# Later reciprocals, later sums: moving four small pieces of work in a fused attention and feed-forward kernel

## The chip, the cores and the metric

The kernel runs on one core of one Trainium2 chip. The metric is the device time of one execution in microseconds. Before the change three runs took 1024.36, 1024.68 and 1027.38 us; the median is 1024.68.

## The reference

Three stages follow each other. The first is causal attention over 4 batches, 8 heads, 576 positions and 64 values a head, with a bias from running sums:

```
s_pos  = max(s, 0);  cum = cumsum(s_pos)            # per head, along the positions
scores = q @ k.T / 8 + min(-(cum_q - cum_k), 0)     # -1e9 above the diagonal
attn   = exp(scores - max) / (sum + 1e-9)
x      = attn @ v                                   # heads side by side: 2304 x 512
```

The second stage is `(h - tanh(h)) @ w_out` with `h = x @ w_in` (512 to 2048 to 512). The third is `((x @ w1) * (x @ w2)) @ w3 @ w_out` (512 to 1024 to 512). All is in float32.

## The kernel before

The first part of the kernel runs attention and half of the second stage, woven into each other. The second part runs the other half, multiplies w3 by the last weights, and runs the third stage. Weights come in as pairs of 32-bit words of 64-bit numbers; VectorE puts each tile together with three instructions (L76, L78, L80), ScalarE rounds it and GpSimd takes the difference (L62, L63). Two buffers hold raw tiles, one for a w_in tile (raw_win) and one for a w_out tile (raw_wout) at a time, so that a load waits for the conversion before it.

Attention works on 32 pairs of heads. A pair of kind A covers the first 256 queries in one unit of work; a pair of kind B covers the other 320 queries in three units (B1, B2, B3). Pairs 0 to 3 are of kind A and pairs 4 to 7 of kind B, all of batch 0. From pair 8 on the kinds take turns. `k0` is the step at which a pair's first unit is scored; its units are two steps apart, and `ke` is the step of the last.

The order on TensorE is written by hand. Each piece of work is entered with `at(step, order, function)`; steps run upward, and the order number sorts within a step. Filling matmuls (`warm`, L187, three a step) stand in steps 0 to 11. For a pair the entries are:

- `scores` (L201, for batch 0 also L216) at the unit's step; `minimum` (row maxima, L228 to L232) and `exps` (L257, L258 or L261) one step later.
- `invert` (L304, L305) at `ke + 2`: VectorE adds 1e-9 to the row sums and takes reciprocals into `rw`.
- `turn` (L309) at `ke + 3`: TensorE transposes `rw` into a bank named `pri`.
- `store` (L314, L316) at `ke + 4`: ScalarE copies `pri` to `rt`, and SP writes it to a small tensor `rd` in device memory.
- `spread` (L322) at `ke + 6`: SP reads `rd` back twice, each over 64 partitions, into `rb`.
- `transposes`, `evacuate` and `products` (L272, L281, L298) some 5 to 9 steps after the scores; `finish` (L335) at `ke + lag + 3`, where `lag` is 5 for the first four pairs and 7 for the rest: VectorE multiplies the product by `rb` into `xy`.

`scores`, `transposes`, `turn`, the products of most pairs and `queries` take their bank from one pool of five (`ps_a`). A bank comes free when its last reader is done.

For batch 0 the bias is made on TensorE. It needs `rel2`: for each of five chunks of queries the running sums less the sum at the chunk's start, in a rounded part (L556) and a correction (L557). VectorE makes all ten at the start, in the order of chunks 0, 1, 3, 4, 2. Pairs 0 to 3 use chunks 0 and 1; pair 4 uses chunk 3 at step 8, chunk 4 at step 10 and chunk 2 at step 12. `queries` (L562, L565) transposes the running sums into a bank `pcq` and copies them to `cq`, which batches 1 to 3 use from step 30 on.

The second stage enters steps as units of six matmuls (`ffn`). When a block of 256 tokens may begin follows from the `finish` steps: the first at step 14, the second at step 40. The code spreads the units over the steps between.

VectorE, ScalarE, GpSimd and SP are not ordered by hand: a planner gives each a fixed order from its own estimate of when each instruction can run, and the engines then take their instructions in that order.

Of the kernel before, what the change touches and what calls it, by code (L numbers as in the profile page):

```python
# [37 lines left out]
def tile_kernel(ctx: ExitStack, tc: tile.TileContext, qk, v, s, w_in, w_out, w1, w2, w3t, w_o2, outT):  # L38
# [65 lines left out]
    with ExitStack() as actx:  # L104
# [355 lines left out]
        def at(step, order, fn, *args):  # L460
            when.setdefault(step, []).append((order, len(when.get(step, ())), fn, args))
# [10 lines left out]
        for p in pairs:  # L472
            n, k0 = p.n, k
            lag = 5 if p.first and p.early else 7
            for m, j in enumerate(p.units):
                k = k0 + 2 * m
                for i in NEED[j]:
                    at(max(k - 2, start), 5, bias, p, i)
                    if not p.first:
                        at(max(k - 1, start + 1), 0.2, causal, p, i)  # L480
                at(k, 4, scores, p, j)
                at(k + 1, 1, minimum, p, j)
                at(k + 1, 2.5, exps, p, j)
                for e in range(2):
                    at(k + e + lag, 2, transposes, p, j, e)
                    at(k + e + lag + 1, 1.5, evacuate, p, j, e)
                at(k + lag + 2, 8, products, p, j)
            ke = k0 + 2 * len(p.units) - 2
            k = ke + 2
            at(ke + 2, 5.5, invert, p)  # L490
            at(ke + 3, 2.4, turn, p)
            at(ke + 4, 1.2, store, p)
            at(ke + 6, 3.9, spread, p)
            fin = ke + lag + 3
            at(fin, 2.6, finish, p)
            if p.hp == H // 2 - 1:
                avail.append((S * p.b + (BLK if p.early else S), fin))

            if n > 1 and (p.early or p.first):
                q = p if p.first else pairs[n + 1]  # L500
                at(max(k0 - 6, start + 1), 4.2, load, p, q, "load")
                at(max(k0 - 2, start + 1), 4.3, load, p, q, "load_v")
                if not p.first:
                    at(k0 - 5, 4.4, load, p, pairs[n + 1], "load_cum")
# [43 lines left out]
        for z in range(2):  # L548
            for y in range(2):
                nc.gpsimd.tensor_copy(rel2[z][2 * NH:, 512 * y:512 * y + 512], zeros[2 * NH:])  # L550
        for i in (0, 1, 3, 4, 2):
            z, r = REL[i]
            w = min(P * (i + 1), S)
            base = cum[:, CH0[i] - 1:CH0[i]] if i else 0.0
            hi, lo = rel2[z][:NH, r:r + w], rel2[z][NH:2 * NH, r:r + w]
            nc.vector.tensor_scalar(out=hi, in0=cum[:, :w], scalar1=base, scalar2=None, op0=ALU.subtract)  # L556
            nc.vector.scalar_tensor_tensor(out=lo, in0=cum[:, :w], scalar=base, in1=hi.bitcast(F32), op0=ALU.subtract, op1=ALU.subtract)  # L557

        def queries():
            pt = ps_a.tile([P, 512], F32, tag="s", name="pcq")  # L560
            for i in range(5):
                nc.tensor.transpose(pt[:PW[i], NH * i:NH * i + NH], cum[:, CH0[i]:CH0[i] + PW[i]], ident[:NH, :NH])  # L562
            for i0, i1 in ((0, 3), (3, 5)):
                pw = PW[i0]
                nc.vector.tensor_scalar(out=cq[:pw, i0:i1], in0=pt[:pw, NH * i0:NH * i1].rearrange("p (i g) -> p i g", g=NH),  # L565
                                        scalar1=-1.0, scalar2=None, op0=ALU.mult)

        at(12, 5.2, queries)

        ff = ffn()  # L570
        alive = True
# [193 lines left out]
```

## Time and profile before

| | |
|---|---|
| median of three runs | 1024.68 us |
| profiled execution | 1030.51 us |
| its span | 1028.2 us |
| TensorE busy (PE) | 974.8 us, 95% |
| VectorE busy (DVE) | 524.5 us, 51% |
| ScalarE busy (ACT) | 394.7 us, 38% |
| GpSimd busy (POOL) | 253.8 us, 25% |
| mean granted TensorE clock | 0.972 |

Times inside the profile count from the start of the span. A row of the timeline has start, duration, engine, line, operation and tiles; the square bracket at its end is the idle time of the engine before it and what ended that. A granted clock of 1.00 is full speed.

### The profile page before, as it was taken

How to read it: one execution, taken by the hardware profiler on the slowest of the kernel's cores; microseconds unless marked ns; L12 is line 12 of the kernel's file. 1: busy time of each engine (PE TensorE's matmuls, PEld its weight loads, DVE VectorE, ACT ScalarE, POOL GpSimd, SP SyncE). 2: the span in 40 equal slices, each digit the busy share in tenths (PEclk: the TensorE clock that was granted, in tenths of full speed). 3: DMA queues.
4: the chain of work that ended last, by engine and by line, in shares of the span. 5: the costliest groups of instructions: out<-in, count | busy, mean ns of one | idle time of the engine just before them, and what ended most of it. 6: DMA issues, size and time to landing. Idle time of an engine off the chain costs nothing.

```text
span 1028.2 us, 15378 instructions
## 1 busy us (share of the span) xinstructions
PE 974.8 (95%) x5809; PEld 795.6 (77%) x5809; DVE 524.5 (51%) x1173; ACT 394.7 (38%) x978; POOL 253.8 (25%) x249
## 2 busy tenths in 40 slices
PE   5877898999999999999988999999999999999998
PEld 2544676668787878999867878889888888888898
DVE  8885645755656664642696575657312213122121
ACT  2555566676666654311432333232212112121121
POOL 3332565654433330100332322232101001000000
PEclk7879899999999999999998999999999999999999
DMA  6656745652222310135358361629800101001010
GB/s 201 205 184 231 237 148 175 207 205 83 94 73 99 106 67 31 62 101 186 118 164 272 103 221 61 211 101 341 335 1 1 41 1 41 1 1 42 1 41 21
DMA packets 46234, 123.64 MB, mean 120 GB/s; under 512 B 4977, under 2 KB 16913, under 8 KB 46161
## 3 DMA queue, kind: packets, MB, share of 16 engines
q1 hardware_dynamic: 41840, 106.94, 30.6%
q10 hardware_dynamic: 4320, 15.73, 4.6%
q8 instruction: 45, 0.74, 0.3%
q14 instruction: 29, 0.23, 0.1%
HBM read 92.09 MB, written 30.56 MB: 119 GB/s over the span
## 4 chain that ended last, share of the span: by engine, by line
PE 49%; DVE 6%; DMA 3%; ACT 1%; issue 1%; POOL 0%; SPq 0%; ACTq 0%; POOLq 0%; DVEq 0%
PE oc L100 10%; PE a L100 10%; PE b L100 10%; PE hb L100 6%; PE yb L100 6%; PE w3o L100 4%; PE h L100 2%; PE y L402 2%; DVE cvt_w L78 1%; DVE glb L63 1%; DVE x L63 1%; DMA raw_w<-in_w3t 1%; DVE cvt_w L76 1%; DMA win<-wf_d 1%; DVE cvt_wo L78 1%
## 5 line engine op out<-in xcount | busy, mean ns | idle before, releaser
L100 PEld LDWEIGHTS h<-xhl,win 128*128 128x128 f32 x864 | 111.5, 193 | 30.7 <-issue 12.6
L100 PE MATMUL h<-xhl,win 128*128 128x256 f32 x864 | 126.8, 293 | 8.5 <-DVE th L433 7.1
L712 DVE TENSOR_TENSOR pc<-b,pc 128x512 f32<-128x512 f32 (+1 forms) x40 | 25.5, 637 | 163.3 <-PE b L100 163.3
L100 PE MATMUL hb<-x,win 128*128 128x512 f32 (+1 forms) x480 | 106.8, 369 | 1.5 <-DMA win<-wf_d 1.5
L100 PE MATMUL a<-y,w 128*128 128x512 f32 (+1 forms) x480 | 106.4, 368 | 0.0
L100 PE MATMUL b<-y,w 128*128 128x512 f32 (+1 forms) x480 | 106.0, 368 | 0.0
L100 PE MATMUL yb<-ghb,wout 128*128 128x512 f32 (+1 forms) x320 | 99.1, 376 | 5.6 <-ACT ghb L62 3.7
L100 PEld LDWEIGHTS hb<-x,win 128*128 128x128 f32 x480 | 84.5, 189 | 17.0 <-DMA win<-wf_d 1.7
L100 PE MATMUL oc<-phc,w3s 128*128 128x512 f32 (+1 forms) x320 | 96.7, 368 | 0.0
L100 PEld LDWEIGHTS b<-y,w 128*128 128x128 f32 x480 | 84.3, 189 | 15.0
L100 PEld LDWEIGHTS a<-y,w 128*128 128x128 f32 x480 | 84.2, 189 | 14.9
L180 POOL TENSOR_SCALAR pr<-cb,cq 128x384 f32<-128x384 f32 (+1 forms) x48 | 86.2, 1813 | 9.5 <-DMA cb<-cum_d 5.7
L402 PE MATMUL y<-gh,wout 128*128 128x256 f32 x576 | 88.1, 292 | 0.0
L402 PEld LDWEIGHTS y<-gh,wout 128*128 128x128 f32 x576 | 74.7, 191 | 6.5 <-issue 5.1
L261 ACT ACTIVATE pr<-pr,nm 128x128 f32<-128x128 f32 (+2 forms) x120 | 71.4, 598 | 20.5 <-DVE nm L239 20.1
L63 POOL TENSOR_TENSOR y<-xy,y 128x512 fp32r<-128x512 f32 (+1 forms) x10 | 13.5, 1356 | 248.8 <-ACT y L62 248.6
L711 ACT COPY pc<-a 128x512 f32<-128x512 f32 (+1 forms) x40 | 21.8, 544 | 134.8 <-PE a L100 134.8
L100 PEld LDWEIGHTS yb<-ghb,wout 128*128 128x128 f32 x320 | 59.6, 192 | 17.8 <-ACT ghb L62 4.3
L201 PE MATMUL s_B<-qk 64*96 64x512 f32 (+2 forms) x256 | 60.2, 531 | 12.2 <-ACT pr L257 6.7
L100 PEld LDWEIGHTS oc<-phc,w3s 128*128 128x128 f32 x320 | 58.5, 189 | 9.9
L100 PE MATMUL yb<-glb,wout 128*128 128x512 f32 (+1 forms) x160 | 59.7, 377 | 1.7 <-DVE glb L63 1.7
L62 ACT CAST phc<-pc 128x512 fp32r<-128x512 f32 (+1 forms) x40 | 23.1, 578 | 93.2 <-DVE pc L712 93.2
(129 smaller groups left out, 1646.6 us busy)
## 6 DMA issues: line engine op xcount, KB each, us to landing
qk<-in_qk SPq DMA_DIRECT2D x16, 576.0 KB
raw_w<-in_w3t SPq DMA_DIRECT2D x16, 512.0 KB
raw_w<-in_w SPq DMA_DIRECT2D x16, 512.0 KB
wg_d<-park_w SPq DMA_DIRECT2D x16, 512.0 KB
w<-wg_d SPq DMA_DIRECT2D x16, 512.0 KB
raw_win<-in_w_in ACTq DMA_DIRECT2D x15, 512.0 KB
raw_wout<-in_w_out ACTq DMA_DIRECT2D x15, 512.0 KB
cb<-cum_d SPq DMA_DIRECT2D x12, 576.0 KB
```

What stands on the lines that cost most here:

```text
L62: (hi or nc.scalar.copy)(dst_hi, src)
L63: (lo or nc.gpsimd.tensor_sub)(dst_lo, src, dst_hi.bitcast(F32))
L76: nc.vector.tensor_scalar(out=t, in0=r3[:, :, 1], scalar1=3, scalar2=0x3FFFFFFF, op0=ALU.logical_shift_left, op1=ALU.bitwise_and)
L78: nc.vector.scalar_tensor_tensor(out=t, in0=r3[:, :, 0], scalar=29, in1=t, op0=ALU.logical_shift_right, op1=ALU.bitwise_or)
L100: nc.tensor.matmul(ps, a, b, start=first and n == 0, stop=last and n == 2, skip_group_check=skip)
L180: nc.gpsimd.tensor_scalar(out=t[:pw, e, :w], in0=p.cb[:pw, e, :w], scalar1=c, scalar2=0.0, op0=ALU.add, op1=ALU.min)
L201: latest[0] = nc.tensor.matmul(ps[e][:PW[i], o:o + k1 - k0], x[:, 0, CH0[i]:CH0[i] + PW[i]], x[:, 1, k0:k1], start=(i, k0, k1, o) == UNITS ...
L261: nc.scalar.activation(t[:pw, :], t[:pw, :], AF.Exp, bias=m, scale=-1.0, accum_out=p.sums[:pw, e, c:c + 1])
L402: nc.tensor.matmul(o, wout[f][:, z, P * c:P * c + P], x, start=f == 0 and n == 0 and c % 2 == 0, stop=f == F1 - 1 and n == 2, skip_group_c ...
L711: nc.scalar.copy(t[:, :n], pa[:, :n])
L712: nc.vector.tensor_mul(t[:, :n], pb[:, :n], t[:, :n])
```

## The change

`turn` moves from `ke + 3` to `ke + 5`, `store` from `ke + 4` to `ke + 6`, into the step of `spread`. `finish` of the first four pairs moves one step. With it the first block of the second stage may begin at step 15. Of the ten instructions on `rel2`, the six of chunks 3, 4 and 2 are entered at steps 2, 3 and 4, and `queries` moves from step 12 to step 22.

```diff
-            at(ke + 3, 2.4, turn, p)
-            at(ke + 4, 1.2, store, p)
+            at(ke + 5, 2.4, turn, p)
+            at(ke + 6, 1.2, store, p)
             at(ke + 6, 3.9, spread, p)
-            fin = ke + lag + 3
+            fin = ke + lag + (4 if p.first and p.early else 3)
...
-        for i in (0, 1, 3, 4, 2):
+
+        def relative(i):
             z, r = REL[i]
             w = min(P * (i + 1), S)
             base = cum[:, CH0[i] - 1:CH0[i]] if i else 0.0
             hi, lo = rel2[z][:NH, r:r + w], rel2[z][NH:2 * NH, r:r + w]
             nc.vector.tensor_scalar(out=hi, in0=cum[:, :w], scalar1=base, scalar2=None, op0=ALU.subtract)
             nc.vector.scalar_tensor_tensor(out=lo, in0=cum[:, :w], scalar=base, in1=hi.bitcast(F32), op0=ALU.subtract, op1=ALU.subtract)
+
+        for i in (0, 1):
+            relative(i)
+        for z, i in enumerate((3, 4, 2)):
+            at(2 + z, 5.6, relative, i)
...
-        at(12, 5.2, queries)
+        at(22, 5.2, queries)
```

## Rows read from the trace of the kernel before

**Rows 1.** The page's slices of 25.7 us, in tenths: TensorE busy, granted clock.
```profile
PE   5877898999999999999988999999999999999998
...
PEclk7879899999999999999998999999999999999999
```

**Rows 2.** TensorE's waits, 0 to 130 us: total us, times, longest.
```profile
PE pri L309 <- DVE nm L232: 8.0, 1, 8.0
...
PE s_B L201 <- issue: 4.6, 1, 4.6
```

**Rows 3.** Timeline of TensorE around the first transposition of reciprocals.
```profile
20.88 0.45 PE L309 MATMUL pri<-ident,rw 128*96 128x128 f32 x1 [7.98 <-DVE nm L232]
21.12 1.49 PE L187 MATMUL spare<-zeros,identb 128*128 128x512 bf16 x3
22.53 1.65 PE L201 MATMUL s_A<-qk 64*128 64x128 f32 x8
```

**Rows 4.** Stretches: length, busy us of PE, PEld, DVE, ACT, POOL, clock, DMA, GB/s.
```profile
10.00:54.00 44.00, 30.70 (x174) 18.01 (x172) 36.68 (x83) 19.77 (x62) 15.03 (x15) 0.79 0.61 190
...
20.90:33.50 12.60, 11.37 (x49) 6.99 (x50) 10.70 (x22) 6.49 (x24) 4.67 (x4) 0.64 0.57 173
...
250.00:450.00 200.00, 199.40 (x1615) 168.45 (x1614) 115.36 (x366) 108.18 (x302) 58.78 (x63) 1.00 0.22 71
```

**Rows 5.** Timeline of VectorE before pair 0's reciprocals.
```profile
17.57 0.43 DVE L76 TENSOR_SCALAR cvt_win<-raw_win 128x512 uint32<-128x512 uint32 x1 [2.81 <-DMA raw_win<-in_w_in]
...
20.65 0.17 DVE L305 RECIPROCAL rw<-rw 128x4 f32<-128x4 f32 x1
```

**Rows 6.** VectorE's waits, 10 to 54 us.
```profile
DVE cvt_win L76 <- DMA raw_win<-in_w_in: 4.9, 4, 2.8
```

**Rows 7.** Tile rel, VectorE's instructions: ns least, median, most; first and last start; forms.
```profile
L556 DVE TENSOR_SCALAR rel<-cum x5: 215/402/501, 5.8 to 7.0; 32x128 fp32r<-32x128 f32 x1, 32x256 fp32r<-32x256 f32 x1, 32x512 fp32r<-32x512 f32 x1, 32x576 fp32r<-32x576 f32 x1
L557 DVE SCALAR_TENSOR_TENSOR rel<-cum,rel x5: 280/602/801, 7.5 to 9.5; 32x128 fp32r<-32x128 f32 x1, 32x256 fp32r<-32x256 f32 x1, 32x512 fp32r<-32x512 f32 x1, 32x576 fp32r<-32x576 f32 x1
```

**Rows 8.** Timeline around pair 5's first scores.
```profile
54.03 0.38 DVE L565 TENSOR_SCALAR cq<-pcq 128x96 f32<-128x96 f32 x2
...
54.51 1.99 PE L201 MATMUL s_B<-qk 64*96 64x512 f32 x2 [4.60 <-issue]
...
58.13 2.02 PE L201 MATMUL s_B<-qk 64*96 64x512 f32 x2 [1.63 <-ACT pr L257]
```

**Rows 9.** Timeline of ScalarE's queue: first and last of six requests for raw_win.
```profile
12.77 0.38 ACTq L67 DMA_DIRECT2D raw_win<-in_w_in  x1
...
52.08 0.33 ACTq L67 DMA_DIRECT2D raw_win<-in_w_in  x1
```

**Rows 10.** Timeline: a pair's reciprocals copied, stored, spread and used.
```profile
22.82 0.24 ACT L314 COPY rt<-pri 4x128 f32<-4x128 f32 x1
...
37.34 0.41 DVE L335 TENSOR_TENSOR xy<-pv,rb 128x256 f32<-128x256 f32 x1
...
41.19 0.64 SPq L316 DMA_DIRECT2D rd<-rt  x1
...
45.73 1.11 SPq L322 DMA_DIRECT2D rb<-rd  x2
...
160.22 0.64 SPq L316 DMA_DIRECT2D rd<-rt  x1
...
166.63 1.12 SPq L322 DMA_DIRECT2D rb<-rd  x2
...
176.74 0.42 DVE L335 TENSOR_TENSOR xy<-pv,rb 128x256 f32<-128x256 f32 x1 [1.29 <-PE pv L298]
```

**Rows 11.** Timeline: a conversion on VectorE beside a subtraction on GpSimd.
```profile
21.39 1.27 POOL L63 TENSOR_TENSOR win<-cvt_win,win 128x512 fp32r<-128x512 f32 x1 [5.50 <-ACT win L62]
21.50 1.71 DVE L80 SCALAR_TENSOR_TENSOR cvt_wout<-raw_wout,cvt_wout 128x512 uint32<-128x512 uint32 x1
```

**Rows 12.** Timeline of TensorE: a later transposition of reciprocals.
```profile
181.61 0.28 PE L309 MATMUL pri<-ident,rw 128*96 128x128 f32 x1 [2.03 <-DVE rw L305]
```

## The prediction

> **What bounds the kernel now.** I read the page's slices first, then TensorE's waits, then the timeline of the places they name, then stretches of both engines. Of the forty slices TensorE's busy share is five to eight tenths in six of the first seven, and nine in nearly all that follow; the granted clock is below full in the same early slices [rows 1]. From 250 to 450 us it works 199.4 of 200 us [rows 4]. So nothing later makes up for time lost early, and time won early reaches the end, as long as the stages between carry it on.
>
> The largest wait of TensorE is one: 8.0 us before the transposition of pair 0's reciprocals (pri) [rows 2]. Its order is written by hand, and at step 3 this transposition stands ahead of the scores of pair 2. The engine stands still for 7.98 us up to 20.88, and pair 2's scores start at 22.53 [rows 3]. What it waits for is VectorE: the reciprocal runs at 20.65, behind a conversion that had itself waited 2.81 us for its raw weights [rows 5]. After the stall the clock is low: the mean is 0.64 from 20.9 to 33.5 us, between the levels 1.2 and 2.4 GHz [rows 4].
>
> But VectorE is the fuller engine there. From 10 to 54 us it works 36.7 of 44 us, TensorE 30.7 [rows 4]. VectorE takes its instructions in order, and 4.9 us of its 7.3 idle us are waits for the next raw_win [rows 6]. The conversions and the row maxima before step 12 are the same work after the change. So the reductions of pair 4's last chunk can come earlier by 7.3 us at most if the same work stands before them, however early TensorE has the scores ready.
>
> **The change part by part.** The profiled execution took 1030.51 us (span 1028.2 and 2.3 around it), 5.83 above the median of 1024.68. I work in us saved against that execution and take the same number from the median.
>
> *Transposition at the pair's last step plus 5 in place of 3.* TensorE's next work at step 4, three filling matmuls and pair 2's scores, no longer has the reciprocal ahead of it. It needs two of the five banks that pairs 0 and 1 hold or leave free, and gets the second when pair 0's exponentials are done, which the reciprocal needs as well. Removed: up to 7.98 us of stall. Late next is VectorE, so the value is what fills VectorE's idle time, counted after the next edit.
>
> *Sums of chunks 3, 4 and 2 at steps 2, 3 and 4.* These are three subtractions and three corrections (L556, L557). By median and longest of each five, the 384-wide ones take 0.40 and 0.60 us, the 576-wide ones 0.50 and 0.80, the 512-wide ones about 0.47 and 0.72: 3.5 us [rows 7]. They now stand before the first conversion and the first row maxima. Without them both come up to 3.5 us earlier, the second load of raw_win is asked for earlier, and the moved work has a place in the 2.81 us that VectorE idles [rows 5]. From both sides: a gain of 3.5 us if all finds idle time, and a loss of 3.5 if the planner of the engines' order puts it in front of the row maxima of pair 1. I take 2.8, the size of that gap, since the gap stands right behind the work of that time.
>
> *Together, up to step 12.* Of the 7.3 us, 2.8 are spent; 4.5 are left. Pair 2's row maxima no longer wait for TensorE and may fill such gaps, but a wait for raw_win holds everything behind it. I take a third: 1.5 us (between 0 and 4.5).
>
> *The queries at step 22 in place of 12.* TensorE waits 4.60 us before pair 5's first scores, which start at 54.51 when VectorE has copied pcq (54.03) out of its bank [rows 2, 8]. Without pcq they start up to 4.6 us earlier. But the second half waits for a bank of pair 4 whose exponentials (L257) are still to come, and starts at 58.13; that stays. Left is the copy's 0.38 us, which stood in VectorE's order before the last row maxima were scaled: 0.3 us. At step 22 the bank is taken while two chunks, not three, have theirs; cost between 0 and one such copy, taken as 0.
>
> *Later pairs.* At 181.61 TensorE waits 2.03 us for another reciprocal (L305) [rows 12]. Two steps later that wait is over. VectorE's backlog stays, so I count half: 1.0 (0 to 2.03).
>
> *The moved work beside GpSimd.* The corrections run now while GpSimd rests. Beside the conversions they can meet its subtractions of weights. One VectorE conversion beside such a subtraction took 1.71 us against GpSimd's 1.27 [rows 11], while a correction of the same kind takes 0.28 to 0.80 alone [rows 7]. Between 0 and three times 1.27, 3.8 us. GpSimd works 4.67 of the 12.6 us from 20.9 to 33.5 [rows 4], a share of 0.37; three corrections that meet it by that share and wait half a subtraction each pay 0.7, which I take.
>
> The Trainium skill ("SBUF — State Buffer", section "Who interferes with whom") says that a VectorE instruction with two SBUF inputs and a GpSimd instruction that reads SBUF take one shared port, and whichever starts second waits for the whole of the other. By it each correction started inside a subtraction pays the rest of that subtraction, which the 1.71 us agrees with. What it makes of the sum is rival D.
>
> *Finish one step later for the first four pairs, and block 0 of the feed-forward work from step 15.* Worked through the code's loop, the 288 units end at step 168 in both, and from step 66 on each step has the same number. The units before that move by one step at most: 0. The copy (0.24 us) moves with its step: 0.
>
> *Store and spread in one step.* SP takes its instructions in order, and a spread holds SP until its store has landed; 160.22 to 166.63 is the longest case [rows 10]. Behind it stand loads of pairs asked for six steps ahead. I count 0; what it does to finish is the third rival.
>
> Sum: 2.8 + 1.5 + 0.3 + 1.0 − 0.7 = 4.9 us. 1024.68 − 4.9 = 1019.8 (1025.6 for an execution like the profiled one).
>
> **Rivals.**
>
> *A: TensorE sets the pace.* If conversions are planned later, past step 12, VectorE's 7.3 us is no bound; from 54 us on it has idle time. Then the whole 7.98 comes back. The clock comes back too: 11.37 busy us at 0.64 [rows 4] would take 7.3 at full clock, 4.1 less. With 2.0 and 0.3 that is 14.4 us: 1010.3. For it: the low clock and the filling matmuls, 1.49 us for three at 21.12 [rows 3]. Against it: VectorE's share.
>
> *B: the loop of weight loads sets the pace.* A raw_win can be asked for only when the one before is converted. Six requests go from 12.77 to 52.08 [rows 9], 7.86 us a round, and the transposition is no part of a round. If the sixth conversion still stands before pair 4's last row maxima and the moved sums fall between conversions, step 14 comes when it came. Left are 0.3 and 1.0: 1023.4. For it: 4.9 us of waits for raw_win. Against: the gap of 2.81 is the first round's, and the first conversion can start earlier.
>
> *C: the reciprocals come too late (slower).* Finish multiplies in VectorE's order, so a late spread stops row maxima and holds a product's bank. Pair 0's reciprocals are copied at 22.82 and used at 37.34: 14.5 us over four steps [rows 10]. Now there are three steps: 10.9, or 9.0 if a step shrinks to 3 us. The way there: up to 4.5 us from store to spread (41.19 to 45.73), 1.1 for two issues, and a landing that no row shows, between 0 and the 4.5 of that store: 5.6 to 10.1. Late by up to 1.1 us in each of four pairs. Later pairs of this kind have 16.5 us over six steps (160.22 to 176.74), 11.0 over four; their worst way is 6.4 + 1.1 + 4.5 = 12.0, late by 1.0, in twelve pairs. All of that is 16.4 us; half of it, less the 4.9, is 3.3 us slower: 1028.0. It decides from the point where spreads land after the products. For it: spreads have waited up to 4.5 us for their stores. Against: most pairs have some us in hand.
>
> *D: the moved corrections collide.* All three meet a whole subtraction: 3.8 in place of 0.7, 1022.9. For it: the meeting that cost 1.0 us [rows 11]. Against: GpSimd rests for most of these stretches [rows 4]. The port rule of the Trainium skill ("SBUF — State Buffer", same section) would make this the rule whenever the two overlap.
>
> **How the numbers follow.** My forecast has 0.42, its own range 1016.5 to 1021.6. A has 0.13, B 0.20, C 0.19, D 0.06. A measurement can tell about 0.3% here, 3.1 us. Forecast and A are faster by more: 0.55. B and D lie within: 0.26. C is slower: 0.19. The range runs from 1011, which leaves out about half of A, to 1028, which leaves out about half of C.
>
> **What would show it.** Right: no wait of TensorE before pri of over 1 us; pair 2's scores by 17 us, ahead of pair 0's pri; moved sums in VectorE's order between 10 and 25 us, its first wait for raw_win under 1 us; pair 5's first half no longer behind pcq, its second half still behind L257; pair 4's last row maxima near 48.5 in place of 52.8. For A: those maxima before 46, a granted clock of 1.00 through 20 to 34 us. For B: the same raw_win spacing and a start, and pair 5's second half still at 57 to 58. For C: VectorE waiting for rb before L335. For D: corrections of over 1.2 us. I am wrong if the engines' order, planned anew, moves row maxima behind conversions: then no term holds.

## The result, and the profile after

The changed kernel takes 1012.67 us in the median of four runs (1010.10 to 1015.99), the kernel before 1026.03 beside it (four runs, 1024.36 to 1028.14). The ratio is 0.9866, with a 95% interval of 0.9837 to 0.9895: 13.4 us faster, more than twice the 4.9 forecast and near the low end of the range. The profiled execution took 1012.79 us, its span is 1010.1; against the profiled execution of before that is 18.1 us of span, so the profiles show the difference somewhat larger than the medians do.

The page after: span, and the slices that answer to [rows 1].

```profile
span 1010.1 us, 15368 instructions
...
PE   7788899999999999999998999999999999999998
...
PEclk9878999999999999999999999999999999999999
```

The slices differ mainly at the start. To place the difference I split both profiles at two points of TensorE's hand-written order that exist in every kernel here: the start of the scores of the pair of step 40, and of the pair of step 72.

| | to step 40 | step 40 to 72 | from 72 to the end |
|---|---|---|---|
| before | 147.4 | 89.3 | 791.5 |
| after | 139.8 | 80.2 | 790.1 |
| difference | 7.6 | 9.1 | 1.4 |

The stretches of TensorE that this stands on, of before (columns as in [rows 4]):

```profile
0.00:147.38 147.38, 115.79 (x692) 76.51 (x692) 105.63 (x243) 74.37 (x216) 59.18 (x68) 0.85 0.64 207
...
147.38:236.68 89.30, 80.66 (x601) 60.76 (x600) 54.61 (x181) 62.33 (x180) 55.27 (x58) 0.96 0.52 178
```

and of after, with two that answer to [rows 4]:

```profile
10.00:54.00 44.00, 31.89 (x170) 17.38 (x173) 37.58 (x89) 23.40 (x76) 14.08 (x15) 0.85 0.64 199
20.90:33.50 12.60, 10.46 (x53) 5.42 (x55) 10.23 (x27) 8.49 (x34) 5.22 (x8) 0.89 0.68 196
...
0.00:139.78 139.78, 115.11 (x690) 76.37 (x693) 103.26 (x240) 74.50 (x217) 57.58 (x67) 0.87 0.64 210
...
139.78:220.00 80.22, 78.87 (x601) 59.83 (x600) 56.01 (x183) 62.08 (x178) 57.77 (x59) 1.00 0.61 212
```

Length less busy time is TensorE's idle time. Up to step 40 it falls from 31.6 to 24.7 us: 6.9 of the 7.6. From step 40 to 72 it falls from 8.6 to 1.35, 7.3 of the 9.1; the other 1.8 is the same work done faster, at a granted clock of 1.00 in place of 0.96. The gain is mostly idle time removed; from 20.9 to 33.5 us the clock rose from 0.64 to 0.89, but up to step 40 that is worth only 0.7 us of busy time.

**The start.** TensorE's waits from 0 to 130 us after, and its timeline:

```profile
PE s_B L201 <- ACT pr L257: 8.8, 2, 7.0
...
PE pri L309 <- ACT pr L258: 1.5, 1, 1.5
```

```profile
13.18 0.49 PE L201 MATMUL s_A<-qk 64*128 64x128 f32 x2
15.96 0.92 PE L201 MATMUL s_A<-qk 64*128 64x128 f32 x6 [2.29 <-ACT pr L258]
...
21.87 0.32 PE L309 MATMUL pri<-ident,rw 128*96 128x128 f32 x1 [1.50 <-ACT pr L258]
...
51.74 2.02 PE L201 MATMUL s_B<-qk 64*96 64x512 f32 x2 [7.04 <-ACT pr L257]
```

The 7.98 us of [rows 3] are gone. Pair 2's scores start at 13.18; six of the eight wait for a bank until pair 0's exponentials (L258) are done and run at 15.96, as the prediction reasoned. The transposition (pri) still waits 1.50 us. The second half of pair 5 (51.74, before 58.13) still stands behind L257. VectorE after:

```profile
7.12 2.60 DVE L558 SCALAR_TENSOR_TENSOR rel<-cum,rel 32x128 fp32r<-32x128 f32 x5
...
16.91 0.43 DVE L76 TENSOR_SCALAR cvt_win<-raw_win 128x512 uint32<-128x512 uint32 x1 [2.29 <-DMA raw_win<-in_w_in]
...
20.72 1.15 DVE L228 TENSOR_REDUCE nm<-s_A 128x1 f32<-128x128 f32 x4
...
46.77 1.27 DVE L228 TENSOR_REDUCE nm<-s_B 128x1 f32<-128x384 f32 x4
```

All five corrections of `rel` still run at the start (x5 at 7.12; the line numbers moved by one). Pair 4's last row maxima run at 46.77; in the trace of before the same row is

```profile
52.84 1.28 DVE L228 TENSOR_REDUCE nm<-s_B 128x1 f32<-128x384 f32 x4
```

**Steps 40 to 72.** TensorE's waits from 138 to 240 us, before, and then after:

```profile
PE h L100 <- DVE th L433: 5.0, 3, 3.0
PE pri L309 <- DVE rw L305: 2.0, 1, 2.0
PE h L100 <- ACT xhl L62: 1.0, 1, 1.0
```

```profile
PE pt_B L272 <- ACT pf_A L281: 0.9, 1, 0.9
```

The prediction knew only the second of these rows (pri, 2.0 us, [rows 12]). The larger one is a unit of the second stage waiting for VectorE's subtraction of the tanh. Timeline of before around the longest of the three, all engines:

```profile
147.38 0.93 PE L201 MATMUL s_A<-qk 64*128 64x128 f32 x8
...
153.97 0.28 SPq L316 DMA_DIRECT2D rd<-rt  x1
155.22 0.45 SPq L322 DMA_DIRECT2D rb<-rd  x1
...
156.36 0.41 SPq L164 DMA_DIRECT2D cb<-cum_d  x1
156.60 0.33 ACTq L67 DMA_DIRECT2D raw_wout<-in_w_out  x1
...
159.77 0.68 DVE L80 SCALAR_TENSOR_TENSOR cvt_win<-raw_win,cvt_win 128x512 uint32<-128x512 uint32 x1
159.94 0.25 ACT L314 COPY rt<-pri 4x128 f32<-4x128 f32 x1
163.41 3.54 POOL L180 TENSOR_SCALAR pr<-cb,cq 128x384 f32<-128x384 f32 x2 [5.69 <-DMA cb<-cum_d]
164.53 0.33 ACTq L67 DMA_DIRECT2D raw_win<-in_w_in  x1
164.97 0.38 ACT L430 ACTIVATE th<-h 128x256 f32<-128x256 f32 x1 [4.78 <-issue]
165.86 1.65 PE L100 MATMUL h<-xhl,win 128*128 128x256 f32 x6 [3.04 <-DVE th L433]
```

Two things are late there. ScalarE runs nothing between 160.2 and 164.53, then asks for the next `raw_win`, and only then runs the tanh that VectorE and TensorE wait for. And the running sums for the bias of later pairs (`cb`, 576 KB) are asked for 9.0 us after the scores of step 40, behind a store and a spread of reciprocals; GpSimd, which multiplies them, stands 5.69 us. The same place after:

```profile
139.78 0.93 PE L201 MATMUL s_A<-qk 64*128 64x128 f32 x8
...
145.82 0.43 SPq L164 DMA_DIRECT2D cb<-cum_d  x1
...
148.40 0.28 SPq L316 DMA_DIRECT2D rd<-rt  x1
...
150.38 0.68 DVE L80 SCALAR_TENSOR_TENSOR cvt_wout<-raw_wout,cvt_wout 128x512 uint32<-128x512 uint32 x1
151.09 0.33 ACTq L67 DMA_DIRECT2D raw_wout<-in_w_out  x1
151.53 0.38 ACT L430 ACTIVATE th<-h 128x256 f32<-128x256 f32 x1 [1.20 <-DVE cvt_wout L80]
```

The load is asked for 6.0 us after the scores, ahead of the store, and ScalarE's request goes out as soon as VectorE is done with the buffer.

### The profile page after: what moved, and what is told of

Same layout as the page of the kernel before. It is cut to its first block, busy times and chain, and to the rows that moved or that the text cites. A ratio compares the mean times of both kernels' runs of the same rounds, so it can differ in the third digit from the quotient of the medians.

```text
span 1010.1 us, 15368 instructions
## 1 busy us (share of the span) xinstructions
PE 971.4 (96%) x5806; PEld 793.5 (79%) x5809; DVE 523.5 (52%) x1173; ACT 394.5 (39%) x978; POOL 254.4 (25%) x249
## 4 chain that ended last, share of the span: by engine, by line
PE 50%; DVE 6%; DMA 3%; issue 1%; ACT 1%; POOL 0%; SPq 0%; ACTq 0%; DVEq 0%; POOLq 0%
PE oc L100 10%; PE a L100 10%; PE b L100 10%; PE yb L100 6%; PE hb L100 6%; PE w3o L100 4%; PE h L100 2%; PE y L402 2%; DVE cvt_w L78 1%; DVE glb L63 1%; DVE x L63 1%; DMA raw_w<-in_w3t 1%; DVE cvt_w L76 1%; DVE cvt_wo L78 1%; DMA wg_d<-park_w 0%
## 5 line engine op out<-in xcount | busy, mean ns | idle before, releaser
L180 POOL TENSOR_SCALAR pr<-cb,cq 128x384 f32<-128x384 f32 (+1 forms) x48 | 86.5, 1816 | 14.6 <-PE pt_B L272 9.2
L201 PE MATMUL s_B<-qk 64*96 64x512 f32 (+2 forms) x256 | 62.4, 525 | 14.7 <-ACT pr L257 8.8
```

The lines of the kernel that those rows point to most:

```text
L180: nc.gpsimd.tensor_scalar(out=t[:pw, e, :w], in0=p.cb[:pw, e, :w], scalar1=c, scalar2=0.0, op0=ALU.add, op1=ALU.min)
L201: latest[0] = nc.tensor.matmul(ps[e][:PW[i], o:o + k1 - k0], x[:, 0, CH0[i]:CH0[i] + PW[i]], x[:, 1, k0:k1], start=(i, k0, k1, o) == UNITS ...
```

## The experiments

Ratios are to the kernel before, measured beside each, with 95% intervals; the last three columns are the stages of the one profiled execution. Two executions of one program differ in them by 1 to 2 us: before and `rel_later`, whose engines all have the same order, differ by 1.3 up to step 40 and by 1.8 from step 72 on.

| kernel | median us | ratio | to 40 | 40 to 72 | from 72 |
|---|---|---|---|---|---|
| turn_a0 | 1019.82 | 0.9920 [0.9892, 0.9948] | 140.9 | 85.0 | 790.8 |
| turn_b | 1018.75 | 0.9911 [0.9885, 0.9937] | 147.9 | 79.9 | 788.8 |
| queries_22 | 1025.11 | 0.9957 [0.9930, 0.9984] | 142.6 | 88.4 | 788.5 |
| rel_later | 1027.88 | 0.9990 [0.9969, 1.0010] | 146.1 | 89.7 | 789.7 |
| turn_all | 1012.74 | 0.9844 [0.9818, 0.9869] | 139.0 | 80.9 | 791.9 |
| after_fin3 | 1012.36 | 0.9847 [0.9820, 0.9874] | 137.6 | 82.8 | 790.7 |
| cb_early | 1024.99 | 0.9971 [0.9949, 0.9994] | 149.7 | 82.0 | 790.4 |
| after_cb | 1011.73 | 0.9843 [0.9816, 0.9870] | 138.8 | 79.7 | 790.5 |
| cb_early12 | 1023.73 | 0.9953 [0.9927, 0.9980] | 146.5 | 81.9 | 789.9 |
| after_cb_late | 1029.47 | 0.9997 [0.9968, 1.0025] | 141.9 | 89.8 | 800.3 |
| turn_one | 1022.13 | 0.9923 [0.9893, 0.9953] | 145.6 | 84.1 | 788.4 |
| late_sp | 1022.94 | 0.9943 [0.9917, 0.9970] | 145.3 | 85.0 | 787.8 |
| late_pool | 1024.33 | 0.9954 [0.9929, 0.9979] | 146.8 | 86.5 | 789.6 |
| after_late_sp | 1010.90 | 0.9837 [0.9808, 0.9866] | 132.8 | 81.7 | 790.0 |

### The parts of the change, one at a time

**turn_a0**: the later turn and store for pairs 0 to 3 alone, with their later finish.

```diff
+            off = 2 if p.first and p.early else 0
-            at(ke + 3, 2.4, turn, p)
-            at(ke + 4, 1.2, store, p)
+            at(ke + 3 + off, 2.4, turn, p)
+            at(ke + 4 + off, 1.2, store, p)
...
-            fin = ke + lag + 3
+            fin = ke + lag + (4 if p.first and p.early else 3)
```

> Transposition and store two steps later for pairs 0 to 3 alone, with their finish one step later; all else as before. Theory 1 (two separate gains: about 6 us up to step 32 from pairs 0 to 3, about 11 us between steps 32 and 64 from the later pairs): 6 us less than before, about 1020. Theory 2 (one gain; what comes after step 32 follows from being early): 13 us less, about 1013. Theory 3 (the moved start of the feed-forward work does it): also 13 less here, since the finish moves here too.

**turn_b**: the same for all pairs but those four; finish as before.

```diff
+            off = 2 if not (p.first and p.early) else 0
-            at(ke + 3, 2.4, turn, p)
-            at(ke + 4, 1.2, store, p)
+            at(ke + 3 + off, 2.4, turn, p)
+            at(ke + 4 + off, 1.2, store, p)
```

> Transposition and store two steps later for pairs 4 to 31 alone; the first four pairs and their finish as before. Theory 1: the 8 us wait at pair 0 stays, the gain between steps 32 and 64 is there: 7 to 11 us less than before, about 1017. Theory 2: within 2 us of before. Theory 3: within 2 us of before.

**queries_22**: the queries alone.

```diff
-        at(12, 5.2, queries)
+        at(22, 5.2, queries)
```

> The queries' sums at step 22 in place of 12, all else as before. Theories 1 to 3: the second half of pair 5's first scores still waits for pair 4's exponentials, within 1 us of before. A fourth theory (the bank that pcq held sets the pace of the steps after it): 4 us less.

**rel_later**: the sums of chunks 3, 4 and 2 at steps 2 to 4, alone.

```diff
-        for i in (0, 1, 3, 4, 2):
+        def relative(i):
...
+        for i in (0, 1):
+            relative(i)
+        for z, i in enumerate((3, 4, 2)):
+            at(2 + z, 5.6, relative, i)
```

> The sums of chunks 3, 4 and 2 entered at steps 2 to 4, all else as before. All theories: the planner puts the ten instructions where it put them before, so the time is that of before within 1 us; the prediction's term of 2.8 us would be 2.8 less.

The two halves of the turn act in different places, but not in quite separate ones. The first four pairs win before step 40 (147.4 to 140.9) and 4.3 between steps 40 and 72; the later pairs win nothing before step 40, where they keep the long wait before pri (8.6 us), and all of the second part (79.9). So alone they win 9.4 us between steps 40 and 72, and beside the first four's turn 4.8 (85.0 to 80.2). What is left of TensorE's waits in turn_a0 (138 to 240 us) is mostly the row that the prediction knew, now longer:

```profile
PE pri L309 <- DVE rw L305: 4.4, 3, 2.6
```

The moved sums do nothing: the order of every engine in the built program is that of before, because the planner puts the ten instructions at the start wherever they are entered. The queries alone win some 4 us (0.4%), against 0.3 forecast; that is the figure of the fourth theory.

### The whole turn, without the queries or without the later finish

**turn_all**: the change without the queries and the sums.

```diff
-            at(ke + 3, 2.4, turn, p)
-            at(ke + 4, 1.2, store, p)
+            at(ke + 5, 2.4, turn, p)
+            at(ke + 6, 1.2, store, p)
...
-            fin = ke + lag + 3
+            fin = ke + lag + (4 if p.first and p.early else 3)
```

> The changed kernel with the queries' sums back at step 12: transposition, store and finish as changed, the rest as before. If the three gains seen alone (8, 9 and 4 to 5 us) share the same idle time, this is within 2 us of the changed kernel, about 13 less than before; if the queries' share adds, it is 4 us slower than the changed kernel.

**after_fin3**: the changed kernel with the finish where it was.

```diff
-            fin = ke + lag + (4 if p.first and p.early else 3)
+            fin = ke + lag + 3
```

> The changed kernel with the finish of the first four pairs at its old step, so that the feed-forward units start at step 14 as before; the reciprocals have two steps, not three, from store to use. Rival C (late reciprocals hold VectorE): 2 to 5 us slower than the changed kernel. If neither the finish nor the start of the feed-forward work matters: within 2 us of it.

Both have the time of the change within their intervals. So the turn and the store alone carry the whole gain; what the queries win alone they don't win beside them. In turn_all the first half of pair 5's first scores waits 5.41 us (pcq holds its bank), the second half 1.32 more for L257:

```profile
48.80 1.99 PE L201 MATMUL s_B<-qk 64*96 64x512 f32 x2 [5.41 <-issue]
...
52.10 2.02 PE L201 MATMUL s_B<-qk 64*96 64x512 f32 x2 [1.32 <-ACT pr L257]
```

After, the first half runs at 43.60, and the second waits 7.04 us for L257 and starts at 51.74, only 0.36 us sooner.

### The load of the running sums

**cb_early**: the kernel before, `cb` entered two steps earlier for every pair.

```diff
-                at(k0 - 5, 4.4, load, p, pairs[n + 1], "load_cum")
+                at(k0 - 7, 4.4, load, p, pairs[n + 1], "load_cum")
```

> The kernel before with one edit: the running sums of pairs 8 on (cb) are asked for two steps earlier (seven steps ahead of the scores in place of five). TensorE's order is that of before, the reciprocals' transposition included. Theory 5 (the gain of steps 32 to 72 comes from SP's order: with the later transposition the requests for cb go out ahead of the stores of reciprocals, the bias has its input in time, and ScalarE's tanh behind the bias is not late): 5 to 9 us less than before. Theory 6 (TensorE's own waits for reciprocals and banks make it): within 2 us of before.

**after_cb**: the same edit on the changed kernel.

> The changed kernel with cb asked for two steps earlier as well. Theory 5: the cb waits left in the changed kernel (2.7 to 2.9 us at a time on ScalarE, 5.5 on GpSimd) go, but TensorE is already dense from step 40 on, so 0 to 2 us less than the changed kernel. Theory 6: no difference.

**cb_early12**: the kernel before, two steps earlier only from pair 12 on, whose loads come after step 40.

```diff
-                at(k0 - 5, 4.4, load, p, pairs[n + 1], "load_cum")
+                at(k0 - (7 if n >= 12 else 5), 4.4, load, p, pairs[n + 1], "load_cum")
```

> As cb_early, but only for the pairs scored from step 48 on, so that the steps up to 40, where the first form lost 5 us, keep their loads. TensorE's order is that of before. Theory 5 (late cb makes the loss of steps 40 to 72): 5 to 8 us less than before, steps 40 to 72 in 81 to 84 us in place of 89. Theory 6 (TensorE's waits for reciprocals and banks): within 2 us of before.

**after_cb_late**: the changed kernel, one step later from pair 12 on.

```diff
-                at(k0 - 5, 4.4, load, p, pairs[n + 1], "load_cum")
+                at(k0 - (4 if n >= 12 else 5), 4.4, load, p, pairs[n + 1], "load_cum")
```

> The changed kernel with cb of the pairs scored from step 48 on asked for one step later, so that the stores of reciprocals stand ahead of it in SP's order, as they did before the change. TensorE's order is that of the changed kernel. Theory 5: steps 40 to 72 take 85 us or more in place of 80, 4 to 9 us slower than the changed kernel. Theory 6: within 2 us of it.

With TensorE's order of before, the earlier load wins 7.3 (cb_early) and 7.4 us (cb_early12) between steps 40 and 72. cb_early gives part of it back before step 40, where steps 32 to 40 took 28.5 us against 23.3. With TensorE's order of the change, the later load loses all 9.6 us there and 10.2 more from step 72 on: more than expected. Its request, and ScalarE's waits for it from 138 to 240 us, of after_cb_late:

```profile
155.60 0.54 SPq L164 DMA_DIRECT2D cb<-cum_d  x1
```

```profile
ACT pr L182 <- DMA cb<-cum_d: 9.1, 3, 4.7
```

It goes out 13.7 us after the scores of step 40 (141.9), against 6.0, and ScalarE waits 9.1 us in place of 6.8 in the same window of the changed kernel. TensorE's longest wait there is 3.4 us before pri, for a reciprocal; how the late load leads to it was not traced. So a later load lengthens the stretch with the changed order of TensorE too. after_cb took 79.7 us there, 0.5 less than the change, as both theories allow. But cb_early12 changes more than the load. Its timeline:

```profile
147.50 0.33 SPq L164 DMA_DIRECT2D cb<-cum_d  x1
...
158.63 0.39 ACT L430 ACTIVATE th<-h 128x256 f32<-128x256 f32 x1
...
160.04 0.33 ACTq L67 DMA_DIRECT2D raw_win<-in_w_in  x1
```

The tanh now stands ahead of the request. ScalarE's 4.78 us are gone as well, so this kernel can't tell the late load and ScalarE's wait at its request apart.

**turn_one**: the kernel before, turn and store one step later, not two.

```diff
-            at(ke + 3, 2.4, turn, p)
-            at(ke + 4, 1.2, store, p)
+            at(ke + 4, 2.4, turn, p)
+            at(ke + 5, 1.2, store, p)
```

> The kernel before with transposition and store one step later in place of two. Pair 0's transposition still stands ahead of pair 2's scores, and the store of a B pair still comes ahead of the request for cb. By these two places the wait of 8 us before pri and the cb waits stay: within 2 us of before. Theory 6 (what counts is the time that the reciprocals get): half of the changed kernel's gain or more, 6 us or more less.

The first half came as expected: pri still stands ahead of pair 2's scores.

```profile
20.22 0.45 PE L309 MATMUL pri<-ident,rw 128*96 128x128 f32 x1 [7.03 <-DVE nm L232]
20.60 1.65 PE L201 MATMUL s_A<-qk 64*128 64x128 f32 x8
```

The second didn't: 5.2 us were won between steps 40 and 72, though `cb` is asked for 10.7 us after the scores there (156.25), later than before. The late load alone does not explain that. By its whole time, 0.8% less than before, this run meets theory 6's figure; but cb_early and cb_early12 win 7 us of the stretch with TensorE's order of before, so the reciprocals' time alone does not explain the stretch either. What turn_one does not have is ScalarE's stand: it asks for raw_win at 158.46, no wait before a tanh is put down to "issue", and its queue waits nowhere in the stretch for more than 0.8 us for an earlier transfer before such a request.

### ScalarE's request

The profile shows 4.7 to 4.8 us called "issue" before that tanh in three kernels, before, rel_later and queries_22, which took 88.4 to 89.7. turn_a0 has a shorter stand of the same kind under another label: its queue waits 4.61 us at a request, and the tanh behind it is late by 2.78 us (put down to "DVE nm L239"). In before, VectorE was done with the buffer at 160.45. The built program shows what else the request waits for:

```
L67 DMA raw_wout_4121<-in_w_out 128x1024 [waits DMAHW5_49,DVE_49]
...
L67 DMA raw_win_4284<-in_w_in 128x1024 [waits DMAHW6_49,DMAHW5_49,DVE_49]
```

DMAHW0 to DMAHW7 are eight counters that the transfers of SP's and ScalarE's queues take in turn, and a request waits until the transfer that had its counter before has ended. For raw_win that is raw_wout, asked for at 156.60, beside the pair's q and k, cb, a spread and four stores. The trace of before bears this out: ScalarE's queue stands at this wait from 157.83 to 164.49 (the instructions before it ran on until 160.19), and the last piece of raw_wout lands at 164.47; the other counter that it names was complete at 160.40. In queries_22, rel_later and turn_a0 the wait also ends within 0.05 us of the last landing on the counter. Three runs take the requests off ScalarE.

**late_sp**: the kernel before, these requests on SP. **late_pool**: on GpSimd (`nc.gpsimd`). **after_late_sp**: the changed kernel, on SP.

```diff
-            raws = [load_raw(*late[0][2:], nc.scalar)]
+            raws = [load_raw(*late[0][2:], nc.sync)]
...
-                    raws.append(load_raw(*late[m + 1][2:], nc.scalar))
+                    raws.append(load_raw(*late[m + 1][2:], nc.sync))
```

> The kernel before; the raw words of the weights that are parked (raw_win, raw_wout from the sixth block on) are asked for by SP in place of ScalarE. TensorE's order is that of before. Two theories on the stretch from the scores of step 40 to those of step 72, which took 89.3 us before and 80.2 after. Theory 7: half of it is ScalarE standing at such a request: it is idle from 160.2 to 164.5, asks for raw_win at 164.53, and only then runs the tanh for which VectorE and TensorE wait. Then the stretch takes 84 to 85.5 here, ScalarE has no wait of over 2 us before a tanh in it that the profile calls issue, and its waits for cb stay above 8 us. Theory 5 (late running sums alone): 88 to 90, since cb is asked for no earlier. Up to step 40: 146 to 149 by both.

> As the run before, with GpSimd's queue in place of SP's for these requests, so that neither ScalarE nor SP stands at them. Theory 7: the stretch from step 40 to step 72 takes 84 to 86, the upper end if GpSimd, which multiplies the running sums, pays for its own requests. Theory 5: 88 to 90.

> The changed kernel with the same edit as the first of these runs. There ScalarE's longest wait before a tanh in this stretch is 1.3 us, so by theory 7 nothing is to be won: from step 40 to step 72 within 1.5 us of 80.2, and the time within 0.3% of the changed kernel's. Theory 5: the same, unless running sums are asked for later: then slower.

late_sp took 85.0 us between steps 40 and 72, as theory 7 said. ScalarE's waits in it, and the requests:

```profile
ACT pr L182 <- DMA cb<-cum_d: 8.8, 4, 3.0
ACT th L430 <- PE h L100: 1.4, 2, 0.9
```

```profile
154.23 0.41 SPq L164 DMA_DIRECT2D cb<-cum_d  x1
...
158.88 1.07 SPq L67 DMA_DIRECT2D raw_wout<-in_w_out  x1
160.03 0.42 SPq L67 DMA_DIRECT2D raw_win<-in_w_in  x1
```

The wait before the tanh is gone, `cb` is asked for 8.9 us after the scores, as before, and the waits for it are still there (8.8 us, before 10.2): 4.3 us are won with cb no earlier. late_pool won 2.8 (86.5), half a microsecond past the upper end expected, and GpSimd stood for its own requests for up to 3.7 us. Where ScalarE didn't stand (after_late_sp), the stretch took 81.7: nothing won, as expected. Its time is that of the change within the intervals, so no kernel here clearly beats the change; its 132.8 up to step 40 I can't explain.

The 9.1 us thus have two causes of like size: ScalarE's stand, and how late cb is asked for. Without the stand, and with cb asked for 8.5 to 10.7 us after the scores, the stretch takes 84.1 to 86.5 (turn_one, late_sp, late_pool); where cb is asked for within 7.7 us as well, 79.7 to 82.8. turn_a0 (85.0) has some of each: cb at 8.2 us, the stand of 2.78 us and 4.4 us before pri. Each of these edits also moved other rows of the planned orders, so the line between the parts is good to 1 or 2 us only. `turn` and `store` were never moved one without the other, so what each of the two entries does alone is not shown.

## Why the prediction was wrong

The direction was right and its first step is in the trace: the 7.98 us stall is gone, all of pair 2's scores have started by 17 us, and pair 5's second half still stands behind L257. Other signs did not come: TensorE waits 1.50 us before pri where at most 1 was named, VectorE's first wait for raw_win is 2.29 where under 1 was named, and pair 4's last row maxima run at 46.77, not near 48.5. The sign of being wrong came the other way round: row maxima moved ahead of conversions, not behind them. That the time lies inside the stated range is luck: the range reaches so low for rival A's sake, and no sum had more than 2.0 us for the stretch behind step 40. The size came out otherwise, step by step.

- **Later pairs, 1.0 forecast; 9.4 found alone between steps 40 and 72, 4.8 beside the first four pairs' turn.** This is the step that failed most. It looked at one row, TensorE's 2.03 us before pri [rows 12], and took half. All of it went. But 6.0 us more of TensorE's waits between steps 40 and 72 (5.0 and 1.0) stood before units of the second stage, which the prediction never listed. The longest, 3.04 us, came from ScalarE's stand at a request; 1.48 us at 209.35 followed a wait of ScalarE for cb (4.01 us). "Store and spread in one step ... I count 0" weighed only the loads of q, k and v behind the spread, not cb, and not the requests on ScalarE's queue. Asking for cb ahead of the store, and the turn of the counters that this shifts, made most of the second part of the gain, as far as the runs separate it.
- **Moved sums, 2.8 forecast, 0 found.** They did not move. VectorE's order is planned, and the entry's step is no due time for work that is ready. The price of −0.7 for their meeting GpSimd fell with them; the longest correction takes 0.80 us.
- **Pair 2's row maxima, 1.5 forecast; with the above, 7.6 up to step 40.** The bound of 7.3 us rested on "if the same work stands before them". It doesn't: ten weight conversions now stand ahead of pair 4's last row maxima; before it was eleven and two of the three instructions of the twelfth. That the planner did so because pair 2's and pair 4's scores come earlier is the likely reason, not a tried one. From the first conversion to those maxima VectorE works 31.5 us in place of 35.4 and idles 5.5 in place of 7.3, so of the 6.1 us that they come earlier 3.9 are less work and 1.8 idle time. Its idle time for raw_win stayed (5.2 us against 4.9 from 10 to 54 us, the first wait 2.29).
- **Queries, 0.3 forecast.** Beside the turn they win nothing that can be measured, for the reason given: the wait passes to L257. Alone they won 4 us; up to step 40 the profile shows 4.8 against before and 3.5 against rel_later, which has the orders of before. Why is open.
- **Finish and block 0, 0 forecast.** after_fin3 agrees.

Of the rivals, **A** named the mechanism of the start, conversions planned later, and its time of 1010.3 is nearer than the forecast. But its signs came only in part: 46.77 for the maxima, where it asked for under 46, and a clock of 0.89, not 1.00. And on the stretch behind step 40 it put only the 2.0 us of the one row. **B** saw the round of raw_win rightly and drew the wrong end from it. Six requests after, first and last:

```profile
12.62 0.38 ACTq L67 DMA_DIRECT2D raw_win<-in_w_in  x1
...
51.30 0.33 ACTq L67 DMA_DIRECT2D raw_win<-in_w_in  x1
```

That is 7.74 us a round against 7.86: the loop runs as it did, and the row maxima have moved ahead of a turn of it. **C** did not come. VectorE's group at the finish, of after (busy, mean ns, idle and what ended most of it):

```profile
L335 DVE TENSOR_TENSOR xy<-pv,rb 128x256 f32<-128x256 f32 (+2 forms) x48 | 15.6, 353 | 16.0 <-PE pv L298 15.6
```

Of 16.0 idle us 15.6 end with the product, so at most 0.4 with rb. **D** could not come, since the corrections stayed alone; the port rule of the Trainium skill ("SBUF — State Buffer", section "Who interferes with whom") was not put to the test by any run here.

## What to carry to other kernels

Where some engines' orders are planned, an entry moved on the hand-ordered engine replans the others: list which instructions each planned engine, the DMA queues included, now takes in another order before pricing a wait, since the bound from one engine's idle time holds only for an unchanged order. When a move changes the place of a store that waits in an in-order queue, price what stood behind it on that queue. And read every wait of the stretch, not the one that carries the moved instruction's name: here the named row was 2.0 us of 8.6 idle.

## What the runs showed that I had not expected

- A request for a transfer can hold a compute engine with nothing in the profile to name it. ScalarE stood 4.1 us at a load after its buffer was free, and the profile calls it "issue"; the wait ended 0.02 us after the transfer before it on the same counter had landed.
- Asked for at 156.36 in a crowd of transfers, a load of 576 KB was first used at 163.41, 7.05 us later; asking 7.7 us later (13.7 against 6.0 after the scores) cost 9.6 us in that stretch alone.
- The granted clock of a stalled stretch rose from 0.64 to 0.89 (20.9 to 33.5 us), and busy time up to step 40 changed by only 0.7 us.
